# Two of twelve token pairs loaded with four tokens to a partition, and a new order of all steps, in a fused gated-attention and feed-forward kernel

## The chip, the core and the metric

The kernel runs on one core of a Trainium2 chip. The metric is device microseconds (us) from the first to the last instruction of one execution, with what lies around it. Five engines work beside each other, each through its own queue in order: TensorE (PE in the profile; its weight loads are PEld), VectorE (DVE), ScalarE (ACT), GpSimd (POOL) and SyncE (SP), which issues nearly all DMAs. A step that waits holds up everything behind it on its engine.

## What is computed

```
f = 1 / (1 + exp(-f_logit))                          # 4 batches, 8 heads, 768 tokens, 48 channels
for t in range(768):
    state = f[t][:, None] * state + outer(k[t], v[t])  # 48 x 48 for each batch and head
    y[t]  = q[t] @ state
x = y with the heads side by side                    # 3072 tokens x 384
h = x @ w_in                                         # 384 -> 2048
out = (h * cos(h)) @ w_out                           # 2048 -> 384
```

## The kernel before

**Attention.** The recurrence is worked in chunks of 128 tokens, two chunks (256 tokens of one batch) at a time; such a pair is the unit of the loop, and there are twelve, three to a batch. A pair lies on 128 partitions with two consecutive tokens on each, so a chunk takes 64 partitions, and all eight heads lie along each row. `fetch` and `load` (L296) bring f, k, q and v; a run of bytes in DRAM is 2 tokens x 48 channels x 4 bytes = 384 bytes. For pair n the steps are: `ex`, `ln` (L329, L333, ACT) give log(1+exp(-f_logit)), the negative log of the gate; `cum` (L374, L380, PE) sums it along a chunk with a triangular matrix and, with the matrix `half`, over whole chunks; `eb` and `ei` (L391, L395, ACT) take the exponentials of the sums with both signs; `fx`, `fy`, `qa`, `ka` (L347, L344, L341 or L338, L351) correct q and k for the two tokens that share a partition; `qm`, `km` (L404, POOL or DVE) multiply q and k by the decays and write bf16; `vb` and four copies `vt` (L197, a helper that records every copy) bring v to bf16 and into the layout in which the two tokens of a partition are apart. `tq`, `tk` (L435) turn q and k on PE, `qkt` copies them out of PSUM; for pairs 5 to 11 a DMA turns them instead. `sc` (L456) makes the scores, `am` (L461, DVE) masks them, `ps` (L479) makes the outer products of a chunk, `st` (L497) adds the state before and `sz` (L503) scales the sum with the decay of the whole chunk; `y` and `yi` (L531) make the output from the masked scores and from the state, `xe` copies it to the x of the second half.

**Pairs 0 and 1** are cut into two halves of the heads (`HALVES`), so that the first heads can start while the others are still on their way: loads, `ex`, `ln`, `fx`, `cum`, `eb`, `ei`, `qa`, `ka` come in two pieces of 4 heads, named .0 and .1.

**Feed-forward.** Units 0 and 1 take 128 tokens each (both of pair 0), unit 2 the 256 of pair 1, and so on. `h` (L579) multiplies x by w_in into two-bank PSUM tiles of 1024 columns (a unit of 128 tokens has two such tiles, one of 256 has four; a step such as h0.01 is half a tile), `co` (L584, ACT) takes the cosine, `g` (L561, DVE) the product, `o` (L595) multiplies by w_out in four steps for each 128 tokens, `ot` copies the result out and `out` (L606) stores it. The weights are fetched in eight pieces of 768 KB (`w0.*` of w_in, `w1.*` of w_out, L282) and cast by `wc` on POOL or ACT. h0.01 needs `wc0.1`, h0.00 `wc0.0`, h0.11 `wc0.3`, h0.10 `wc0.2`.

**The order.** ORDER is a list of all 953 steps with the engine and the buffers of each, written out; every engine runs its steps in that order. The letter after the colon names the engine (T is PE, S ACT, V DVE, G POOL, Y SP), the digits the slots or the PSUM banks. `zf` steps (L264, 54 of them, ZEROS) are matmuls of zeros that fill TensorE's idle time before the feed-forward part runs dense. PSUM has eight banks, and a step that writes a bank waits until its last reader is through.

Of the kernel before, what the change touches and what calls it, by code (L numbers as in the profile page):

```python
# [16 lines left out]
C = 128  # L17
# [8 lines left out]
HALVES = (0, 1)  # L26
VHALVES = ()
# [12 lines left out]
zf12:T2 zf13:T2 zf14:T2 zf15:T2 zf16:T2 zf17:T2 tk0.0:T2 eb0.1:S0 ex1.0:S ln1.1:S1 ln1.0:S fx1.0:S  # L40
q0.1:Y0 q0.0:Y v0:Y0 fx1.1:S eb0.0:S qa0.1:V zqk.1:V qm0.1:V vb0:S0 f3:Y2 k1.1:Y1 km0.1:V qa0.0:V
zf18:T3 cum1.1:T3 zf19:T4 zf20:T4 zf21:T4 tq0.1:T0 cum1.0:T1 qm0.0:G zsz.2:G eb1.0:S1 vt0.3:S2
k1.0:Y ei1.0:S0 ex3:S zf22:T4 zf23:T4 zf24:T4 zf25:T4 zf26:T4 ps0.1:T4,5 ps0.0:T tk0.1:T v1:Y1 f2:Y0
qkt0.1:V0 eb1.1:S ln3:S0 ei1.1:S ka1.0:G q1.0:Y0 tq0.0:T ka1.1:G km1.1:G0 zvt.1:G vt0.0:S ad3:G1
vt0.1:G q1.1:Y vb1:S1 qkt0.0:V1 vt0.2:G zsz.1:G ex2:S w0.1:Y0 w0.0:Y1 k3:Y0 q3:Y1 w0.3:Y2 ln2:S1
vt1.2:S1 fy3:S zf27:T6 zf28:T6 zf29:T6 zf30:T6 zf31:T6 zf32:T6 sc0.0:T0 sz0.01:V2 sz0.00:V w0.2:Y3
ad2:G0 vt1.0:G km1.0:V vt1.3:G wc0.1:G am0.0:V0 zf33:T6 zf34:T6 yi0:T4 sc0.1:T2 am0.1:V1 st0.11:V
sz0.11:V3 wc0.0:G k2:Y1 zf35:T6 zf36:T6 zf37:T6 zf38:T6 ps1.1:T6,7 tk1.0:T0 ps1.0:T zf39:T1 zf40:T1
zf41:T1 cum3:T1 fy2:S ei3:S0 fx3:S ka3:G eb3:S2 vt1.1:S fx2:S km3.0:G1 qa3:G qm3.0:G km3.1:G qm3.1:G
w1.0:Y0 qa1.0:V st0.10:V qa1.1:V qm1.0:V wc0.2:G ka2:G q2:Y2 tk1.1:T2 zf42:T3 zf43:T3 y0:T3 tq1.0:T  # L50
xe0.1:S0 sz0.10:V st1.00:V st1.01:V qm1.1:V v2:Y1 zf44:T5 zf45:T5 zf46:T5 zf47:T5 zf48:T5 tq1.1:T
cum2:T1 sz1.00:V1 qkt1.0:V0 eb2:S0 xe0.0:S ei2:S1 qkt1.1:V1 km2.0:G0 km2.1:G zf49:T5 sc1.0:T4
sz1.01:V zf50:T0 zf51:T0 sc1.1:T2 h0.01:T0 st1.11:V sz1.11:V2 am1.1:V0 wc1.0:G qa2:G zf52:T6 zf53:T6
h0.00:T co0.0:S0 qm2.1:G am1.0:V1 h1.01:T2 h1.00:T co1.0:S1 y1:T6,4 yi1:T g0.0:V1 xe1.1:V1 st1.10:V
qm2.0:G vb2:G1 sz1.10:V g1.0:V4 w1.2:Y3 xe1.0:S tk3.0:T5 h2.01:T0 tq3.0:T w1.3:Y0 qkt3.0:V0 v3:Y0
f4:Y0 h2.10:T6 h2.00:T sc3.0:T4 tq3.1:T2 tk3.1:T h2.11:T wc1.2:G wc1.3:G vt2.1:G1 wc0.3:S vb3:G0
# [48 lines left out]
o16.3:T sc10.0:T2 co10.2:S1 out13:Y ot16:S3 g10.2:V sc10.1:T4 ps11.1:T1 vt11.0:G vt10.3:G2 ps11.0:T
qa11:G vt11.1:S qm11.1:G st11.01:V tq11.1:Y2 sz11.01:V2 am10.0:V0 am10.1:V1 h10.31:T6 o17.3:T0
# [82 lines left out]
def describe(nc, cpool, ppool, q, k, v, f_logit, moe_w_in, moe_w_out, out):  # L189
# [19 lines left out]
    if nc is not None:  # L209
# [3 lines left out]
        for t in (incl, strict, half):  # L213
            nc.vector.memset(t, 0.0)
# [503 lines left out]
```

## Time and profile before

| what | value |
|---|---|
| median of 3 runs | 183.65 us (183.43 to 183.81) |
| the profiled execution | 183.05 us |
| its span, first to last instruction | 181.3 us |
| mean granted TensorE clock | 0.998 |
| PE busy | 174.0 us, 96% of the span |
| DVE, ACT, POOL busy | 138.2, 130.7, 109.2 us |

Matmuls are pipelined and their ends are modelled, so the busy time of a few short matmuls counts some latency twice; the distance between the starts of two groups is the surer measure. A row of the timeline is: start, duration, engine, line, operation, tiles, count, and in brackets the idle time before it and what ended that.

### The profile page before, as it was taken

The numbers are of one execution on the slowest core, as the hardware profiler recorded it, in microseconds if no ns is written. First come the engines' busy times: TensorE is split into PE (matmuls) and PEld (weight loads), VectorE is DVE, ScalarE is ACT, GpSimd is POOL, SyncE is SP. The second block draws the span as 40 slices with busy tenths as digits, with TensorE's granted clock in tenths as the row PEclk, the third lists the DMA queues.
The fourth block names the chain that finished last, engine by engine and source line by source line (L and its number), as shares of the span: only waits on it lengthen the run. The fifth ranks groups of instructions, "written<-read, shape, count | busy, mean of one in ns | idle before, by whom it ended". The sixth has DMA issues, their size and how long they took to land.

```text
span 181.3 us, 5818 instructions
## 1 busy us (share of the span) xinstructions
PE 174.0 (96%) x2464; PEld 124.2 (69%) x2464; DVE 138.2 (76%) x206; ACT 130.7 (72%) x187; POOL 109.2 (60%) x139
## 2 busy tenths in 40 slices
PE   7999788999999999999999999999999999999992
PEld 2555357785677876778657886658788767786661
DVE  5359988898685989897999698689888994466260
ACT  3985988778877999989997899769768452473221
POOL 4229889999969996989755968790799000000000
PEclk9999999999999999999999999999999999999999
DMA  6999999999999945996889999749929400110313
GB/s 141 261 261 263 346 304 318 293 283 281 317 264 241 270 77 128 253 230 133 125 162 317 189 242 253 175 125 244 216 85 197 90 4 0 38 52 4 130 43 130
DMA packets 72282, 33.93 MB, mean 187 GB/s; under 512 B 65344, under 2 KB 70720, under 8 KB 72256
## 3 DMA queue, kind: packets, MB, share of 16 engines
q1 hardware_dynamic: 71584, 33.27, 76.6%
q8 instruction: 19, 0.31, 0.7%
q10 hardware_dynamic: 672, 0.30, 0.6%
q14 instruction: 7, 0.06, 0.1%
HBM read 25.17 MB, written 4.72 MB: 165 GB/s over the span
## 4 chain that ended last, share of the span: by engine, by line
PE 80%; DMA 8%; SPq 5%; DVE 3%; POOL 1%; issue 1%; ACT 1%; POOLq 0%
PE ps L595 35%; PE ps L579 32%; DMA k<-in_k_dram 5%; PE ps L531 5%; SPq L296 3%; PE ps L456 3%; DMA v<-in_v_dram 3%; PE ps L479 2%; DVE g L561 1%; SPq L282 1%; PE ps L435 1%; PE ps L374 1%; DVE am L461 1%; POOL qk L404 1%; POOL k L351 1%
## 5 line engine op out<-in xcount | busy, mean ns | idle before, releaser
L561 DVE TENSOR_TENSOR g<-ps,co 128x1024 bf16<-128x1024 f32 x48 | 61.3, 1311 | 15.8 <-ACT co L584 14.8
L595 PE MATMUL ps<-w_out_bf,g 128*128 128x384 bf16 x384 | 68.9, 326 | 0.0
L579 PE MATMUL ps<-x,w_in_bf 128*128 128x256 bf16 (+1 forms) x624 | 68.2, 264 | 0.6 <-DVE x L197 0.5
L584 ACT ACTIVATE co<-ps,halfpi 128x1024 bf16<-128x1024 f32 x48 | 52.7, 1113 | 20.0 <-PE ps L579 19.8
L579 PEld LDWEIGHTS <-w_in_bf 128*128 128x128 bf16 x624 | 56.3, 98 | 9.3 <-DVE x L197 0.7
L595 PEld LDWEIGHTS <-g 128*128 128x128 bf16 x384 | 36.0, 98 | 21.5 <-issue 0.3
L461 DVE TENSOR_TENSOR am<-ps,pmask 128x1024 bf16<-128x1024 f32 x24 | 28.7, 1218 | 5.0 <-PE ps L456 4.8
L404 POOL TENSOR_TENSOR qk<-k,bi 128x384 bf16<-128x384 f32 x22 | 22.0, 1010 | 5.4 <-ACT bi L391 4.7
L404 POOL TENSOR_TENSOR qk<-q,b 128x384 bf16<-128x384 f32 x21 | 20.9, 1004 | 2.7 <-DVE q L338 2.1
L197 POOL COPY vt<-vb 64x384 bf16<-64x384 bf16 x33 | 16.7, 507 | 1.6
L264 PE MATMUL ps<-zero 128*128 128x512 bf16 x54 | 16.1, 426 | 1.2 <-DVE zero L203 1.2
L503 DVE TENSOR_TENSOR sz<-ps,b 64x192 bf16<-64x192 f32 x40 | 14.1, 353 | 2.5 <-PE ps L479 1.6
L341 POOL TENSOR_TENSOR q<-f,q 128x384 f32<-128x384 f32 x10 | 10.0, 1000 | 8.3 <-DMA q<-in_q_dram 6.1
L363 POOL TENSOR_TENSOR sp<-ls 128x384 bf16<-128x384 f32 x10 | 10.2, 1015 | 7.7 <-ACT ls L333 5.9
L329 ACT ACTIVATE f<-f 128x768 f32<-128x768 f32 (+1 forms) x14 | 10.4, 746 | 4.5 <-DMA f<-in_f_logit_dram 4.4
L351 POOL TENSOR_TENSOR k<-k,f 128x384 f32<-128x384 f32 (+1 forms) x12 | 11.1, 930 | 4.2 <-DMA k<-in_k_dram 4.2
L497 DVE TENSOR_TENSOR ps<-ps,sz 64x192 f32<-64x192 f32 x32 | 11.7, 366 | 1.9 <-PE ps L479 0.8
L197 ACT COPY ot<-ps 128x384 f32<-128x384 f32 (+1 forms) x14 | 6.1, 453 | 8.7 <-PE ps L595 8.7
L197 ACT CAST x<-ps 128x384 bf16<-128x384 f32 x12 | 5.5, 479 | 5.9 <-PE ps L531 5.9
L456 PE MATMUL ps<-qkt 48*64 48x128 bf16 (+1 forms) x304 | 8.7, 219 | 1.0 <-DVE sz L503 0.8
L197 DVE CAST x<-ps 128x384 bf16<-128x384 f32 x12 | 6.4, 552 | 4.0 <-PE ps L531 3.8
L264 PEld LDWEIGHTS <-zero 128*128 128x128 bf16 x54 | 4.9, 105 | 6.1 <-issue 2.2
(64 smaller groups left out, 167.5 us busy)
## 6 DMA issues: line engine op xcount, KB each, us to landing
v<-in_v_dram SPq DMA_DIRECT2D x12, 384.0 KB, 6.0
out_dram<-ot SPq DMA_DIRECT2D x22, 192.0 KB, 2.1
f<-in_f_logit_dram SPq DMA_DIRECT2D x10, 384.0 KB, 6.0
k<-in_k_dram SPq DMA_DIRECT2D x10, 384.0 KB, 6.7
q<-in_q_dram SPq DMA_DIRECT2D x10, 384.0 KB, 6.7
g<-in_moe_w_in_dram SPq DMA_DIRECT2D x4, 768.0 KB, 7.6
g<-in_moe_w_out_dram SPq DMA_DIRECT2D x4, 768.0 KB, 5.8
k<-in_k_dram SPq DMA_DIRECT2D x4, 192.0 KB, 4.5
```

What stands on the lines that cost most here:

```text
L197: (nc.scalar.copy if e == "ACT" else eng(e).tensor_copy)(out=o, in_=i)
L264: G.step(f"zf{i}", ("PE",), lambda e, dump=dump: nc.tensor.matmul(dump.ap, lhsT=zero[:, 0:128], rhs=zero, start=True, stop=True), writes=[ ...
L351: eng(e).tensor_mul(out=w.ap[:, :, 0, :], in0=w.ap[:, :, 0, :], in1=t.ap[:, :, 0, :])
L404: G.step(f"{nm}{n}.{u}", ("POOL", "DVE") if cut else ("POOL",), lambda e, u=u, j=j, src=src, dec=dec: eng(e).tensor_mul(out=qkp[u][j].ap[: ...
L456: nc.tensor.matmul(o[t0:t1, r, 2 * a + g, :].rearrange("p (e n) -> p e n", e=2), lhsT=wide[s, t0 // 64, :] if turned else wide[s].rearrang ...
L461: G.step(f"am{n}.{u}", ("DVE",), lambda e, u=u, sc=sc: nc.vector.tensor_mul(out=am[u].ap.rearrange("p r b n -> p (r b) n"), in0=sc.ap.rear ...
L497: nc.vector.tensor_add(out=view()[s], in0=view()[s], in1=S0.ap[s, :, r, :])
L503: eng(e).tensor_mul(out=new.ap[s, :, r, :].rearrange("p (u a) n -> p u a n", u=2), in0=view()[s].rearrange("p (u a) n -> p u a n", u=2), i ...
L561: nc.vector.tensor_mul(out=o.rearrange("p b (n e) -> p b e n", e=2), in0=ph.ap.rearrange("p (b e n) -> p b e n", e=2, n=64), in1=co.ap.rea ...
L579: nc.tensor.matmul(ph.ap[:, i * T:(i + 1) * T].rearrange("p (g t) -> p g t", t=C), lhsT=w_in_bf[:, kk, f0:f0 + 128], rhs=xa[:, :, kk, :], ...
L584: G.step(f"co{m}.{j}", ("ACT",), lambda e, ph=ph, co=co: nc.scalar.activation(out=co.ap, in_=ph.ap, func=AF.Sin, bias=halfpi), reads=[ph], ...
L595: nc.tensor.matmul(po.ap[:, 0:DM], lhsT=gT.ap[:, j, i * C:(i + 1) * C], rhs=w_out_bf[:, j, :], start=(po.first and j == 4 * s), stop=(po.f ...
```

## The change

It has four parts.

1. **Layout of pairs 0 and 1** (`QUADS`, new function `lead4`). Four consecutive tokens lie on a partition, so a run in DRAM is 768 bytes and a chunk of 128 tokens takes 32 partitions. Heads 0 to 3 of both chunks lie on partitions 0 to 63, heads 4 to 7 on 64 to 127. f, k, q and v of these pairs come as two loads of 192 KB each, one for each half of the partitions (16 loads; before, f, k and q came in two loads each and v in one, 14 in all).
2. **Sums on TensorE.** `cum` sums for each of the four tokens of a partition with its own triangle (`incl4` where the other token counts in, else `strict4`), 8 matmuls of 192 columns for two tokens, and 8 small ones for the totals. So `fx`, `qa`, `ka` are gone for these pairs, `ex` and `ln` are one step each for a pair, and `eb`, `ei` write 384 columns each (two tokens, a half pair), into the slot of f and into two slots of `ot`. `et` is the small exponential of the totals. `tm` spreads the totals with a mask.
3. **v and the state on TensorE.** `vq` spreads v with 16 matmuls against columns of the identity into one two-bank PSUM tile, and one copy `vt` (on DVE in the order) takes it out; before, four copies on ACT and POOL did that. `st` becomes `si`: 8 matmuls that add the state before into the PSUM of the outer products, with `sz` after it on all 128 partitions.
4. **A new order** of all steps, 914 of them, with 32 `zf` instead of 54. The pair-2-to-11 code is the same, the `cut` branches are gone, `gate` takes the number of tokens to a partition.

The new functions, cut:

```
load(...): out=val.ap.rearrange("p h e d -> p (h e d)").rearrange("p (h x) -> p h x", x=e*D),
           in_=tok.rearrange("h (p e) d -> p h (e d)", e=e)
fetch(..., quad): for u in range(2): load(f"{kind}{n}.{u}", whole.part(lambda a: a[64*u:64*u+64]), ..., 4*u, 4*u+4, 4)

def cum(x):                                     # lead4: x = 0, 1: tokens 2x and 2x+1
    for y in range(2):
        for e in range(4):
            matmul(pc[x].ap[:, HB*y:HB*y+HB], lhsT=incl4 if e <= 2*x+y else strict4, rhs=sp4()[:, e, :, 0:D], ...)
    if x == 0:
        for a in range(2):
            for e in range(4):
                matmul(<totals, 4 columns>, lhsT=sp4()[:, e, 2*a:2*a+2, :], rhs=quarter, ...)

def spread(e):                                  # vq
    for g in range(2):
        for u in range(2):
            for x in range(4):
                matmul(pv.ap[32*x:32*x+32, 512*g+HB*u:512*g+HB*u+HB], lhsT=ident[:, t], rhs=vb4()[:, x], ...)

def carry(e):                                   # si
    for u in us:
        for i in range(4):
            matmul(ps[g].ap[t, at(u):at(u)+HB//2], lhsT=ident[:, t], rhs=S0.ap[:, 2*u:2*u+2, i//2, :], ...)
```

The start of each queue in the new order (only the steps that the prediction speaks of):

```
SP   f0.1 f1.1 v0.1 v0.0 k0.1 k0.0 f1.0 q0.0 q0.1 k1.0 q1.0 v1.0 k1.1 q1.1 f3 v1.1 f2 w0.1 w0.0 w0.3 w0.2 q3 w1.2 k3 w1.3 k2 q2 f4 w1.0 w1.1
ACT  f0.0 ex0 ln0 ei0.0 ei0.1 eb0.0 ex1 eb0.1 et0 ln1 et1 eb1.0 ei1.1 ei1.0 eb1.1 ex3 vb1 ex2 ln2 ln3 fy3 qkt1.1 eb2 ei2 fx3 ei3 eb3 wc0.0 fx2 co0.0 co1.0 xe1.0
DVE  km0.0 zsp.1 vt0 qm0.0 zsz.0 tm0 qm0.1 sz0.01 qkt0.0 qkt0.1 sz0.00 qm1.0 am0.0 sz0.10 sz0.11 am0.1 qm1.1 xe0.0 qkt1.0 xe0.1 sz1.00 sz1.01 am1.1 sz1.10 sz1.11 am1.0 vt1 xe1.1 g0.0 g1.0 zsp.2 g0.1 g2.0 g2.2 g2.3 g1.1 qkt3.0 qkt3.1 g2.1
POOL zqk.2 vb0 km0.1 km1.1 tm1 zsz.1 km1.0 ad2 ad3 wc0.1 wc0.3 wc0.2 qa3 qm3.0 wc1.2 ka3 km3.1 km3.0 qm3.1
PE   zf0-12 cum0.0 cum0.1 vq0 zf13 tk0.0 zf14-17 ps0.0 tk0.1 ps0.1 tq0.0 zf18 tq0.1 cum1.0 cum1.1 sc0.0 sc0.1 si0.1 zf19-20 tk1.1 zf21 si1.0 yi0 tq1.0 zf22-23 tq1.1 tk1.0 ps1.1 y0 zf24-26 cum2 zf27-29 cum3 ps1.0 zf30 sc1.1 zf31 si1.1 sc1.0 vq1 h0.01 h0.00 h1.00 h1.01 yi1 y1 h0.11 h0.10 h2.01 h2.00 h2.21 h2.20 h2.30 h2.31 h1.11 h1.10 o0.2 tq3.0 h2.10 h2.11 tk3.1 tk3.0 tq3.1 o3.2 sc3.0 o2.3 o2.2 o1.3 sc3.1 o3.3
end  DVE ot20 ot23.0 ot22.1; ACT ot23.1 ot22.0 (before: ACT ot23.0 ot23.1)
```

In the order before, the same places read:

```
SP   f0.1 k0.0 k0.1 f1.1 f1.0 q0.1 q0.0 v0 f3 k1.1 k1.0 v1 f2 q1.0 q1.1 w0.1 w0.0 k3 q3 w0.3 w0.2 k2 w1.0 q2 v2 w1.2
PE   ... zf49 sc1.0 zf50-51 sc1.1 h0.01 zf52-53 h0.00 h1.01 h1.00 y1 yi1 tk3.0 h2.01 tq3.0 h2.10 h2.00 sc3.0 tq3.1 tk3.1 h2.11 h2.20 h2.21 h0.11 sc3.1 h0.10 h1.11 h1.10 h2.30 tk2.1 tk2.0 h2.31 o2.0 tq2.1 tq2.0 o0.0 o3.0 o1.0
```

More of the change, by code (lines that the diff above doesn't have):

```diff
@@ L40 @@
[L40 to L56, printed above, removed]
@@ L116 @@
-out22.1:Y o23.2:T o23.0:T o23.1:T ot23.0:S3 out23.0:Y ot23.1:S out23.1:S
+zvt.2:V zsz.3:V zqk.1:V f0.1:Y0 zsp.0:V f0.0:S ex0:S ln0:S0 f1.1:Y1 v0.1:Y0 v0.0:Y k0.1:Y0 k0.0:Y
+f1.0:Y q0.0:Y0 q0.1:Y zf0:T0 zf1:T0 zf2:T0 zf3:T0 zf4:T0 zf5:T0 zf6:T0 zf7:T0 zf8:T0 zf9:T0 zf10:T0
+zf11:T0 zf12:T0 cum0.0:T0 ei0.0:S0 cum0.1:T1 ei0.1:S1 k1.0:Y1 q1.0:Y1 eb0.0:S v1.0:Y1 k1.1:Y q1.1:Y
+ex1:S eb0.1:S et0:S0 zqk.2:G vb0:G0 zvt.0:V km0.0:V1 zsp.1:V vq0:T2 km0.1:G vt0:V0 qm0.0:V ln1:S1
+zf13:T4 tk0.0:T4,5 zsz.0:V tm0:V0 qm0.1:V zf14:T6 zf15:T6 zf16:T6 zf17:T6 ps0.0:T2,6 tk0.1:T ps0.1:T
@@ new lines @@
+f3:Y2 v1.1:Y tq0.0:T zf18:T1 tq0.1:T cum1.0:T0 et1:S0 eb1.0:S cum1.1:T1 f2:Y0 sz0.01:V0 qkt0.0:V0
+qkt0.1:V1 sz0.00:V sc0.0:T4 w0.1:Y0 w0.0:Y1 ei1.1:S1 ei1.0:S0 eb1.1:S ex3:S vb1:S0 w0.3:Y2 qm1.0:V1
+km1.1:G tm1:G1 zsz.1:G sc0.1:T2 si0.1:T am0.0:V0 sz0.10:V3 sz0.11:V km1.0:G ex2:S ln2:S0 ad2:G1
+zf19:T0 zf20:T0 tk1.1:T1,0 ln3:S1 zf21:T4 si1.0:T6 w0.2:Y3 yi0:T4 ad3:G0 am0.1:V1 qm1.1:V wc0.1:G
+wc0.3:G tq1.0:T wc0.2:G zf22:T5 zf23:T5 tq1.1:T tk1.0:T ps1.1:T2 y0:T5 fy3:S xe0.0:V0 qkt1.1:S0
+qkt1.0:V1 xe0.1:V q3:Y0 zf24:T5 zf25:T5 zf26:T5 cum2:T1 zf27:T5 zf28:T5 zf29:T5 cum3:T4 ps1.0:T
@@ L506, in pair @@
             for r in range(2):
[L507 to L508 removed]
+                G.step(f"sz{n}.{g}{r}", ("DVE",), lambda e, r=r: decay(e, r), reads=[half_of[r], bt], writes=[new.part(None)])
+        for g in gs:
+            new = Val(szS)
+            (state4 if quad else state2)(g, new, before[g])
             state[b] = new
```

416 lines of the change are left out of this document (252 added, 164 removed).

## The prediction

> **What bounds the kernel now.** First the stages: busy time of each engine by windows (columns: window, length, PE busy with its count, PEld, DVE, ACT, POOL, clock, DMA share, GB/s).
>
> ```profile
> 5.00:16.00 11.00, 10.85 (x131) 5.88 (x129) 6.10 (x13) 9.82 (x25) 4.56 (x6) 1.00 1.28 263
> 18.00:20.00 2.00, 1.31 (x43) 0.71 (x38) 1.76 (x6) 1.94 (x3) 1.26 (x4) 1.00 1.01 353
> ...
> 44.00:60.00 16.00, 16.00 (x262) 11.25 (x257) 11.19 (x21) 12.44 (x18) 13.65 (x20) 1.00 1.14 268
> ```
>
> ```profile
> 80.00:100.00 20.00, 20.00 (x378) 14.65 (x377) 18.39 (x26) 18.50 (x29) 14.72 (x18) 1.00 0.88 190
> ```
>
> From 44 us on TensorE has no idle time, and neither layout nor step count changes there. So the end moves by what is gained or lost before 44, plus the tail. Before that PE looks as busy, but with what?
>
> ```profile
> L264 PE MATMUL ps<-zero 128*128 128x512 bf16 x52 | 15.5, 428 | 1.2 <-DVE zero L203 1.2
> ```
>
> 52 of the 54 zero matmuls lie before 24.9 us: the lead-in is a chain through DMA, ACT, DVE and POOL, and PE waits in it. The timeline shows where the lead-in ends and where it is caught up:
>
> ```profile
> 24.91 0.84 PE L579 MATMUL ps<-x,w_in_bf 128*128 128x128 bf16 x12
> ...
> 26.03 2.17 PE L579 MATMUL ps<-x,w_in_bf 128*128 128x128 bf16 x36
> 26.90 1.11 ACT L584 ACTIVATE co<-ps,halfpi 128x1024 bf16<-128x1024 f32 x1 [0.77 <-PE ps L579]
> ...
> 28.10 1.33 DVE L561 TENSOR_TENSOR g<-ps,co 128x1024 bf16<-128x1024 f32 x1 [0.65 <-POOL qk L404]
> ```
>
> ```profile
> 41.69 2.11 PE L595 MATMUL ps<-w_out_bf,g 128*128 128x384 bf16 x12
> 43.74 0.40 PE L456 MATMUL ps<-qkt 48*128 48x128 bf16 x8
> ```
>
> h0.01 starts at 24.91, the first g at 28.10, and at 43.8 PE has done all of h0 to h2, y1, the turns of pairs 3 and 2, sc3 and sixteen second-half matmuls (o2.0, o0.0, o3.0, o1.0). That point is my yardstick: when does the new order have as much done?
>
> **The durations that I use** (line, engine, what, count, busy, mean ns; groups before 44 us).
>
> ```profile
> L329 ACT ACTIVATE f<-f 128x768 f32<-128x768 f32 x2 | 1.7, 838 | 1.9 <-DMA f<-in_f_logit_dram 1.9
> L333 ACT ACTIVATE ls<-f 128x768 f32<-128x768 f32 x2 | 1.7, 842 | 0.0
> L197 ACT CAST vb<-v 128x768 bf16<-128x768 f32 x2 | 1.7, 832 | 1.0 <-DMA v<-in_v_dram 1.0
> L395 ACT ACTIVATE bi<-ps 128x384 f32<-128x384 f32 x2 | 1.0, 493 | 0.0
> L197 ACT COPY qkt<-ps 128x1024 bf16<-128x1024 bf16 x2 | 2.0, 1007 | 0.2 <-PE ps L435 0.2
> L197 ACT CAST w_in_bf<-g 128x1536 bf16<-128x1536 f32 x1 | 1.5, 1484 | 0.0
> L584 ACT ACT_TABLE_LOAD x1 | 1.3, 1283 | 0.0
> ```
>
> ```profile
> L404 POOL TENSOR_TENSOR qk<-k,bi 128x384 bf16<-128x384 f32 x6 | 6.2, 1033 | 4.9 <-ACT bi L391 4.7
> L363 POOL TENSOR_TENSOR sp<-ls 128x384 bf16<-128x384 f32 x2 | 2.2, 1080 | 0.7 <-ACT ls L333 0.7
> L197 POOL CAST w_in_bf<-g 128x1536 bf16<-128x1536 f32 x3 | 4.3, 1464 | 0.1
> ```
>
> ```profile
> L561 DVE TENSOR_TENSOR g<-ps,co 128x1024 bf16<-128x1024 f32 x8 | 10.2, 1314 | 0.7 <-POOL qk L404 0.6
> L461 DVE TENSOR_TENSOR am<-ps,pmask 128x1024 bf16<-128x1024 f32 x6 | 7.1, 1218 | 1.3 <-PE ps L456 1.3
> L197 DVE COPY qkt<-ps 128x1024 bf16<-128x1024 bf16 x6 | 3.9, 678 | 2.2 <-PE ps L435 2.2
> L503 DVE TENSOR_TENSOR sz<-ps,b 64x192 bf16<-64x192 f32 x8 | 2.8, 354 | 0.2
> L497 DVE TENSOR_TENSOR ps<-ps,sz 64x192 f32<-64x192 f32 x6 | 2.2, 366 | 0.3
> L404 DVE TENSOR_TENSOR qk<-q,b 128x384 bf16<-128x384 f32 x3 | 1.6, 532 | 0.0
> L197 DVE CAST x<-ps 128x384 bf16<-128x384 f32 x1 | 0.5, 543 | 0.0
> ```
>
> ```profile
> 4.26 0.94 ACT L329 ACTIVATE f<-f 128x384 f32<-128x384 f32 x2 [1.73 <-DMA f<-in_f_logit_dram]
> ...
> 8.69 0.33 PE L374 MATMUL ps<-sp,incl 128*128 128x192 bf16 x2
> ...
> 8.86 0.24 PE L380 MATMUL ps<-half,sp 128*128 128x2 bf16 x4
> ...
> 8.96 0.81 PE L264 MATMUL ps<-zero 128*128 128x512 bf16 x3
> ...
> 28.13 0.63 PE L531 MATMUL ps<-am,vt 128*32 128x128 bf16 x32
> 28.59 0.51 PE L531 MATMUL ps<-qkt,sz 128*32 128x128 bf16 x24
> ```
>
> **Part by part.** *Loads.* Now the queue of loads is a straight line in time. In the chain of waits v0, eight half loads behind f0, lands at 5.10 + 5.53 = 10.63:
>
> ```profile
> 5.10 5.53 DMA v<-in_v_dram
> ```
>
> 192 KB at 263 GB/s is 0.75 us, and 4.7 for f0 (the second `ex` of the row above starts there) plus 8 x 0.75 is 10.7, so the rule holds: each load costs its bytes, in the order of issue. Of a load into half the partitions the trace has no row. From above: 384-byte runs went at 263 GB/s, the weights' longer ones at 353; the 768-byte runs could reach the latter, 0.56 us for 192 KB. From below: half the partitions, half of 263, 1.5 us. I take the nearest row, the same bytes in 384-byte runs, 0.75 us. From 4.7 on, k0 is complete at 8.5 (5 loads on), q0 at 10.7, f3 at 15.9, v1 at 16.7, f2 at 18.2, and at 353 GB/s w0.1 20.4, w0.0 22.6, w0.3 24.9, w0.2 27.1. f2 goes into f0's slot, which now holds decays until qm0.1 (12.2); SP waits there with the weights queued behind it, hidden as long as the transfers issued ahead (to 16.7) run on.
>
> *Sums.* cum0.0 has 8 matmuls of 192 columns and 8 small ones. Two took 0.17 us from 8.69 to 8.86, four small ones 0.10 to 8.96: 0.9 us, and 0.7 for cum0.1, each with 0.2 to the reader. Before, a pair took 0.54, so PE gets about 1.0 more a pair; the 22 zero matmuls that go, at 0.21 each (three in about 0.6), give 4.7 back. The added vq is 16 matmuls in four column groups: y's 32 took 0.46 from start to start, 14 ns each for 128 columns, so 0.35. An si takes 0.1 by the same pitch, ps twice its matmuls, a turn 8 instead of 4; I take 0.5, 0.25 to 0.4. All of it lies in time that zeros filled; if no gap were left, PE's own work from 6.4 to h0.01 would add up to some 16.5 us with its 19 zeros, to 22.9, so PE is not what sets 24.7. ps of these pairs takes four banks instead of two, which is hidden while the feed-forward part has none yet.
>
> *ACT* drops `fx` (four of 192 columns) and its three vt copies of these pairs, and gets four exponentials of 384 columns a pair for four of 192, qkt1.1 (1.0) and wc0.0 (1.5): it is full from 13.7 on, and what stands late in its queue is late in the kernel. POOL drops three vt, ka1 and pair 3's steps ahead of the casts, so all of w_in is cast by 28.6 instead of 33.1:
>
> ```profile
> 31.64 1.47 POOL L197 CAST w_in_bf<-g 128x1536 bf16<-128x1536 f32 x1
> ```
>
> *DVE* loses ka, qa and 6 `st` (6 x 0.37 = 2.2 us), wins vt0, vt1 (not shown from PSUM at 768 columns; between x at 0.54 and g at 1.31, I take 1.0 each) and two `xe` (0.54 each): no net gain. vt0 stands ahead of qm0.0 in DVE's queue and ends at 10.25 (vq0 at 8.6, zsp.1); q0, at 10.7, hides it; were q there sooner, qm0.0, tq0, cum1 and all of pair 1 would wait for vt0. DVE's set-up gets about 14 short instructions, some 1.5 us, hidden under f0's arrival and `ex`, `ln`; if it isn't, up to 0.5 us is lost. A `gate` that writes every fourth element: from nothing to 0.1 us each, I take nothing, as the elements are as many.
>
> **The walk**, by the queues in their order (us):
>
> | step | waits for | ends |
> |---|---|---|
> | ex0, ln0 (ACT) | f0 4.7 | 6.4 |
> | cum0.0, cum0.1 | ln0 | 7.5, 8.2 |
> | ei0.1, eb0.0, ex1, eb0.1, ln1 | cum0.1 | 11.7 |
> | km0.1 (POOL), ps0.0 (PE) | ei0.1 8.8 | 9.8, 10.4 |
> | qm0.0, qm0.1 (DVE) | q0 10.7 | 11.3, 12.2 |
> | tq0.1, cum1.0, cum1.1 | qm0.1 | 14.4 |
> | et1, eb1.0, ei1.1, ei1.0, eb1.1 | cum1 | 15.95 |
> | ex3, vb1 | f3, v1 | 17.7 |
> | ex2, ln2, ln3 | **f2 18.2** | 20.8 |
> | fy3, qkt1.1, four eb/ei, fx3 | | 24.8 |
> | wc0.0, fx2, table load | w0.0 22.6 | 26.3, 28.1 |
> | ad2, ad3, wc0.1 (POOL) | ln2 19.95 | 23.6 |
> | am0.0 to xe0.1 (DVE) | sc0.0 14.8 | 22.6 |
> | cum3, ps1.0, sc1.1, si1.1, sc1.0, vq1 | ad3 22.1 | 24.7 |
> | h0.01, h0.00, h1.0 | wc0.1; wc0.0 | 28.5 |
> | am1.1, sz, am1.0, vt1 (DVE) | sc1.1 | 27.8 |
> | y1, xe1.1, g0.0 | vt1 | 29.4, 30.0, 31.4 |
>
> Each row adds the durations above to the later of its queue and its wait. So h0.01 starts at 24.7, 0.2 before 24.91, but g0.0 at 30.0, 1.9 after 28.10: y1 and xe1.1 stand ahead of it. What follows is denser, since no h waits for a cast any more. Tiles come free every 1.31 us with DVE: g1.0 32.7, g0.1 34.2, g2.0 35.5, g2.2 36.8, g2.3 38.1, g1.1 39.4, the two qkt3 40.8, g2.1 42.1. PE follows: h0.1 30.8, h2.0 32.2, h2.2 33.5, h2.3 34.8, h1.1 36.2, o0.2 36.9, h2.1 38.4, turns 39.1, o3.2 39.8, sc3.0 40.5, o2.3, o2.2, o1.3 42.5, sc3.1 42.8, o3.3 43.45.
>
> ```profile
> 46.34 3.36 PE ps L595 x20
> ```
>
> By 43.45 six o steps are done where before had four at 43.80: two at 4 x 0.168 make 1.34; the turns of pair 2 (0.9, the two groups of 0.45 before 41.85) are still owed. That is 0.44 us of work and 0.35 of time: **0.8 us gained**. Tail:
>
> ```profile
> 178.04 0.54 ACT L197 COPY ot<-ps 128x192 f32<-128x192 f32 x2 [4.74 <-PE ps L595]
> 178.62 0.36 ACTq L606 DMA_DIRECT2D out_dram<-ot  x1
> ```
>
> Two copies in a row on ACT become one each on ACT and DVE: 0.2 gained. Sum -1.0 on the profiled execution's 183.05, so 182.05; it lies 0.6 below the median of the runs, so I forecast **182.65** for the median.
>
> **Rivals.** *Half-partition loads are slow.* [...] Place: ex2 on ACT, which stands at f2 already at 0.75 us a load; 14 of them lie ahead of f2 after f0, so every 0.1 us above that costs 1.4 us at ln2, ad3 and all below. At half of the best rate of the rows, 353/2, a load takes 1.11 and the price is 5.0; half way there, at 0.93, 2.5: **185.2**, slower. It decides from 0.82 a load on, where the 1.0 is gone. For it: DMA is never idle from 5 to 20 us. Against: w0.3 and w0.2 stand earlier in the queue. [...] Chance 0.33.
>
> *Loads near 353 GB/s.* Then f2 is there at 15.5, ex2 starts behind vb1 at 17.7 and gains 0.5, and the weights come 2.7 earlier; with turns and cum at the short end another 0.6: **181.6**. Chance 0.17.
>
> *DVE hides it.* g0.0 starts 1.9 late, and am, g and qkt keep DVE full to 42; if PE gets no o steps into those gaps, because o0.2 or sc3 wait for banks a tile longer (1.31), 0.8 - 1.31 leaves it **0.3 slower to even, 183.7**. Chance 0.14.
>
> *The clock drops.* With 22 zeros fewer PE has more gaps; the first ten zero matmuls took 0.43 each, twice the 0.21 of later ones, and a spell of 4.5 us at that speed costs about 2: 184.7. In before gaps up to 0.8 us did no harm. Chance 0.04.
>
> ```profile
> 1.19 4.45 PE L264 MATMUL ps<-zero 128*128 128x512 bf16 x10 [1.19 <-DVE zero L203]
> ```
>
> **Numbers.** The forecast has 0.32, from 182.0 to 183.5. A run tells 0.2% (0.37 us) from no change. Faster: the forecast but 0.03, and the quick loads, 0.46 (0.29 + 0.17); within 0.2%: 0.03 and 0.07 of the DVE case, 0.10; slower: slow loads 0.33, 0.07, 0.04, 0.44. The range 181.3 to 185.6 reaches into both load cases and leaves out the slow end beyond 0.96 us a load.
>
> **What would show it.** DMA at 5 to 14 us: 263 GB/s or more is right, under 240 the first rival. ex2 starting by 18.3 with DMA f as releaser; cum0.0 by 6.5; h0.01 by 24.9 and g0.0 at 30; PE without idle from 31. Wrong would be a wait on q0 beyond 10.7, ACT idle ahead of ex3, vb1 or ex2 by over 1 us, or PE idle after 44, where I allow the new order none.

## The result and the profile after

| | before | after |
|---|---|---|
| median | 183.60 us (5 runs, 183.43 to 183.81) | 195.22 us (5 runs, 194.29 to 195.38) |
| ratio | | 1.0622, 95% interval 1.0596 to 1.0648 |
| profiled execution, span | 183.05, 181.3 us | 195.02, 193.0 us |
| mean granted clock | 0.998 | 0.979 |

The kernel became 11.6 us slower; 182.65 was forecast, with 185.6 as the upper end. One later run (experiment 8, 185.47 us, 2.4% above its fastest) counts as slow and is left out of its ratio. First the stages of after, by the same windows view as in the prediction (window, length, busy time and count of PE, PEld, DVE, ACT, POOL, then clock, DMA share, GB/s).

```profile
5.00:10.00 5.00, 3.13 (x44) 2.12 (x42) 1.25 (x6) 3.05 (x5) 0.96 (x2) 1.00 1.13 221
10.00:15.00 5.00, 4.06 (x119) 2.77 (x120) 3.76 (x10) 2.02 (x4) 1.24 (x1) 1.00 1.13 218
...
20.00:25.00 5.00, 3.81 (x102) 2.40 (x102) 2.08 (x4) 3.45 (x5) 0.89 (x1) 0.61 1.06 375
...
36.00:44.00 8.00, 5.55 (x59) 4.50 (x56) 8.00 (x5) 4.29 (x4) 7.77 (x9) 1.00 0.91 236
44.00:60.00 16.00, 11.60 (x115) 7.49 (x116) 15.93 (x13) 12.73 (x15) 7.49 (x12) 1.00 0.88 198
60.00:180.00 120.00, 120.00 (x1844) 90.22 (x1843) 99.08 (x136) 86.66 (x118) 70.24 (x85) 1.00 0.72 154
```

Three places differ from what was expected. The loads run at 218 to 221 GB/s where before had 263. The clock falls to 0.61 between 20 and 25 us. And from 36 to 60 us, where PE was to be dense from 31 on, PE is busy for 17.15 of 24 us while DVE is full (23.93). In the kernel before, PE had no gap to speak of there; its row for 36 to 44 us:

```profile
36.00:44.00 8.00, 7.97 (x103) 6.12 (x100) 7.36 (x7) 6.60 (x8) 7.92 (x8) 1.00 1.04 290
```

From 60 us PE has no idle time in after, so what was lost lies ahead of that. What fills DVE is seen in the groups of its instructions: all of `g`, and those from 62 us on (count, busy us, mean ns).

```profile
L670 DVE TENSOR_TENSOR g<-ps,co 128x1024 bf16<-128x1024 f32 x48 | 69.3, 1502 | 9.7 <-ACT co L693 9.6
```

```profile
L670 DVE TENSOR_TENSOR g<-ps,co 128x1024 bf16<-128x1024 f32 x40 | 50.5, 1308 | 9.7 <-ACT co L693 9.6
```

and the same line in the window up to 62 us:

```profile
L670 DVE TENSOR_TENSOR g<-ps,co 128x1024 bf16<-128x1024 f32 x8 | 18.8, 2472 | 0.0
```

The shape is the same in both, 128x1024 from PSUM to bf16; the eight gates of units 0 to 2, which write every fourth element, take 2.47 us instead of 1.31. That is 8 x 1.16 = 9.3 us on the engine that is full. PE's waits between 24 and 180 us say who stood behind it (us in total, times, longest):

```profile
PE ps L688 <- DVE g L670: 3.3, 4, 1.2
PE ps L515 <- DVE qkt L193: 1.3, 1, 1.3
PE ps L704 <- DVE g L670: 0.9, 1, 0.9
PE ps L486 <- DVE g L670: 0.8, 1, 0.8
...
PE ps L515 <- DVE g L670: 0.5, 1, 0.5
```

These five make 6.8 us, as much as PE idles between 36 and 60 (24 - 17.15), and all of them end with a `g` or with a copy that stood behind `g` in DVE's queue.

The timeline dates the steps of the walk (start, length, engine, line; in brackets the wait before):

```profile
5.36 0.84 ACT L325 ACTIVATE f<-f 128x768 f32<-128x768 f32 x1 [2.53 <-DMA f<-in_f_logit_dram]
...
22.32 0.84 ACT L405 ACTIVATE f<-f 128x768 f32<-128x768 f32 x1 [0.43 <-DMA f<-in_f_logit_dram]
```

```profile
30.62 2.84 PE L688 MATMUL ps<-x,w_in_bf 128*128 128x128 bf16 x48
```

```profile
34.88 4.77 DVE L670 TENSOR_TENSOR g<-ps,co 128x1024 bf16<-128x1024 f32 x2
39.70 11.57 DVE L670 TENSOR_TENSOR g<-ps,co 128x1024 bf16<-128x1024 f32 x5
52.30 2.46 DVE L670 TENSOR_TENSOR g<-ps,co 128x1024 bf16<-128x1024 f32 x1
```

`ex0` starts at 5.36 (forecast 4.7), `ex2` at 22.32 (18.2), h0.01 at 30.62 (24.7), g0.0 at 34.88 (30.0), and g2.1 ends at 54.8 (42.1). So 4.9 us of the delay are there when the gates begin and 7.8 come while they run.

### The profile page after: what moved, and what is told of

It is laid out like the page before. It is cut to its first block, busy times and chain, and to the rows that moved or that the text cites. A ratio compares the mean times of both kernels' runs of the same rounds, so it can differ in the third digit from the quotient of the medians.

```text
span 193.0 us, 6129 instructions
## 1 busy us (share of the span) xinstructions
PE 175.5 (91%) x2618; PEld 126.3 (65%) x2618; DVE 147.2 (76%) x220; ACT 128.9 (67%) x176; POOL 103.3 (54%) x132
## 4 chain that ended last, share of the span: by engine, by line
PE 73%; DVE 10%; DMA 10%; issue 2%; SPq 2%; ACT 1%; DVEq 0%
PE ps L704 31%; PE ps L688 27%; DVE g L670 8%; DMA k<-in_k_dram 6%; PE ps L640 5%; DMA q<-in_q_dram 4%; PE ps L515 3%; PE ps L554 2%; PE ps L271 2%; SPq L303 2%; PE ps L438 1%; PE ps L486 1%; ACT w_in_bf L193 1%; DVE qkt L193 1%; DVE am L520 1%
## 5 line engine op out<-in xcount | busy, mean ns | idle before, releaser
L670 DVE TENSOR_TENSOR g<-ps,co 128x1024 bf16<-128x1024 f32 x48 | 69.3, 1502 | 9.7 <-ACT co L693 9.6
L693 ACT ACTIVATE co<-ps,halfpi 128x1024 bf16<-128x1024 f32 x48 | 52.9, 1113 | 27.3 <-PE ps L688 18.2
L456 POOL TENSOR_TENSOR qk<-k,bi 128x384 bf16<-128x384 f32 x20 | 19.7, 1002 | 1.1 <-ACT bi L447 0.6
L193 POOL COPY vt<-vb 64x384 bf16<-64x384 bf16 x28 | 13.9, 501 | 6.0 <-PE ps L640 3.0
L271 PE MATMUL ps<-zero 128*128 128x512 bf16 x32 | 11.8, 490 | 3.6 <-DVE am L520 1.4
L422 POOL TENSOR_TENSOR k<-k,f 128x384 f32<-128x384 f32 x10 | 10.0, 1002 | 5.7 <-DMA k<-in_k_dram 5.6
L193 DVE COPY ot<-ps 128x384 f32<-128x384 f32 (+1 forms) x12 | 6.2, 522 | 8.3 <-PE ps L704 7.4
L604 DVE TENSOR_TENSOR ps<-ps,sz 64x192 f32<-64x192 f32 x26 | 9.5, 367 | 3.3 <-PE ps L554 2.5
L610 DVE TENSOR_TENSOR sz<-ps,b 64x192 bf16<-64x192 f32 x32 | 11.1, 353 | 0.7
L405 ACT ACTIVATE f<-f 128x768 f32<-128x768 f32 x10 | 8.4, 839 | 2.3 <-DMA f<-in_f_logit_dram 2.3
L447 ACT ACTIVATE bi<-ps 128x384 f32<-128x384 f32 x10 | 4.9, 492 | 6.4 <-PE ps L442 6.3
```

The source lines that it names most:

```text
L193: (nc.scalar.copy if e == "ACT" else eng(e).tensor_copy)(out=o, in_=i)
L271: G.step(f"zf{i}", ("PE",), lambda e, dump=dump: nc.tensor.matmul(dump.ap, lhsT=zero[:, 0:128], rhs=zero, start=True, stop=True), writes=[ ...
L422: eng(e).tensor_mul(out=w.ap[:, :, 0, :], in0=w.ap[:, :, 0, :], in1=t.ap[:, :, 0, :])
L456: G.step(f"{nm}{n}.{u}", ("POOL",), lambda e, u=u, j=j, src=src, dec=dec: eng(e).tensor_mul(out=qkp[u][j].ap[:, :, :, 0:D], in0=swap(src.a ...
L610: eng(e).tensor_mul(out=new.ap[s, :, r, :].rearrange("p (u a) n -> p u a n", u=2), in0=view()[s].rearrange("p (u a) n -> p u a n", u=2), i ...
L670: nc.vector.tensor_mul(out=o.rearrange("p b (n e) -> p b e n", e=E), in0=ph.ap.rearrange("p (b e n) -> p b e n", e=E, n=C // E), in1=co.ap ...
```

## Experiments

Theory: two causes, the gate's write at a step of four elements and the slow loads of half the partitions. Rivals: the fallen clock; something in the new sums or the order. A ratio compares with runs of the kernel before on the same chip, with its 95% interval in brackets; a difference in us to after is one of medians that may come from two chips.

**1. The gate alone, out of the kernel after.** Units 0 to 2 keep PSUM's order in g, and the store puts the rows in order:

```
+ if E == 4:
+     tensor_mul(out=o, in0=<ph, in order>, in1=<co, in order>); return
- dma_start(out=out[r0:r0 + C, c0:c1], in_=oc.ap)
+ rows = out[r0:r0 + C, c0:c1].rearrange("(n e) c -> e n c", e=4)      # units 0 to 2
+ for x in range(4): dma_start(out=rows[x], in_=oc.ap[32 * x:32 * x + 32])
```

> The changed kernel, but the gate product g of units 0 to 2 is written in the order in which it lies in PSUM (unit steps), and the store puts the rows in order, in four pieces of 32 rows. Theory GATE (the product written in steps of four elements, 2.48 instead of 1.31 us, eight times on a full VectorE, makes the larger part of the 11.6 us): g back to about 1.3 us and 186 to 188.5 us. Rival LEAD-IN (the loads into half the partitions and the clock drop make nearly all, and PE could have used the waits on g for other work): 193 us or more. Neither: if g stays above 2 us, it is not the write step.

Measured: 188.39 us, ratio to before 1.0293 (1.0229 to 1.0356): 6.8 us less than after, 6.0 by the two ratios. The eight gates in the window up to 62 us, and the stage in which PE had been idle:

```profile
L671 DVE TENSOR_TENSOR g<-ps,co 128x1024 bf16<-128x1024 f32 x8 | 9.5, 1211 | 0.2
```

```profile
36.00:44.00 8.00, 8.00 (x144) 7.28 (x137) 6.99 (x8) 6.75 (x8) 7.77 (x9) 1.00 0.98 254
44.00:60.00 16.00, 16.00 (x211) 10.37 (x212) 13.74 (x20) 13.85 (x19) 9.74 (x14) 1.00 0.95 218
```

PE's idle time from 36 to 60 us is gone with it.

**2. The gate alone, put into the kernel before**, units 0 to 2 in steps of four (their tokens come out in another order; the work is the same):

```
- def gate(gv, ph, co, T):      ... e=2, n=64
+ def gate(gv, ph, co, T, E):   ... e=E, n=C // E       # E = 4 if m < 3 else 2
```

> The kernel before, with one edit: g of units 0 to 2 is written in steps of four elements instead of two (which leaves the tokens of these units in another order; the work is the same). GATE: g 2.4 to 2.5 us there, VectorE was full from 28 to 43 us, so most of 8 x 1.17 us shows: 190 to 193 us. LEAD-IN: TensorE finds other work, under 186 us.

Measured: 190.85 us, ratio 1.041 (1.0388 to 1.0433), 7.5 us more than before on the same chip. Its gates up to 62 us:

```profile
L561 DVE TENSOR_TENSOR g<-ps,co 128x1024 bf16<-128x1024 f32 x8 | 19.0, 2475 | 0.6 <-POOL qk L404 0.6
```

No load, no sum and no place in the order was touched, so the price belongs to the write alone.

**3. The loads alone**: the sixteen early loads bring the same number of bytes in the same 768-byte runs, but two heads of 512 tokens to all 128 partitions instead of four heads of 256 to 64. They are other tokens than the reference's, the same ones for both pairs, so only the time counts.

```
- load(name, whole.part(lambda a: a[64*u:64*u + 64]), src, b, c, 4*u, 4*u + 4, 4)
+ dma_start(out=<a[:, 4*u:4*u + 4], 128 partitions>, in_=src[b, 4*u:4*u + 2, 0:4*C, :] as "h (p e) d -> p h (e d)")
```

> The changed kernel, but each of the 16 loads of pairs 0 and 1 brings its 192 KB in runs of 768 bytes to all 128 partitions (two of the four slots a row) instead of 64; it reads other tokens, so only the time counts. GATE: 300 GB/s or more from 5 to 12 us, f2 lands at 16 to 17 instead of 22.2, h0.01 starts at 25 to 26 instead of 30.6, and the end moves by about as much: 189.5 to 191.5 us, with g still at 2.48. LEAD-IN: 186 us or less. If the rate stays near 220 GB/s, it is not the number of partitions.

Measured: 190.14 us, ratio 1.0373 (1.0347 to 1.0398), 5.1 us less than after, 4.6 by the two ratios. The windows row of after and then two of this run, `ex2`, and h0.01:

```profile
5.00:20.00 15.00, 10.19 (x213) 6.62 (x212) 8.36 (x21) 7.72 (x15) 4.68 (x6) 1.00 1.16 222
```

```profile
5.00:20.00 15.00, 13.05 (x316) 8.60 (x317) 10.83 (x25) 10.49 (x20) 5.71 (x8) 1.00 1.10 330
...
5.00:10.00 5.00, 4.75 (x57) 2.92 (x56) 2.87 (x9) 2.97 (x6) 1.82 (x2) 1.00 1.06 324
```

```profile
16.81 0.84 ACT L411 ACTIVATE f<-f 128x768 f32<-128x768 f32 x1 [0.38 <-DMA f<-in_f_logit_dram]
```

```profile
24.24 2.84 PE L694 MATMUL ps<-x,w_in_bf 128*128 128x128 bf16 x48
```

Up to 20 us this run moves part of the weights too, so the loads' own rate is better read from 5 to 10 us: 324 GB/s, where after had 221. 192 KB (196,608 bytes) take 0.89 us at 221 to 222 GB/s and 0.61 at 324. SP's issues don't set that rate: in after the loads of k and v landed 5.7 us (median) after they were issued, so several were under way at any time. Whether it helped the rate that both pairs read the same tokens was not tried apart. h0.01 starts 6.4 us earlier.

**4. The clock**: nine zero matmuls more (ZEROS 41), six of them ahead of `tk1.1` and three behind `zf21`.

> The changed kernel with nine zero matmuls more between 16.7 and 20 us, where TensorE waits and after which its clock falls to half from 21.1 to 28.0 us. If the clock drop costs time of its own: the clock stays at 1.0 and the end comes 1.5 to 3 us earlier, 192 to 193.7 us. If it lies beside the waits for the late loads: within 0.5 us of 195.2, whatever the clock does.

Measured: 194.95 us, ratio 1.0636 (1.0606 to 1.0667). The windows of after, then of this run (the clock is the third number from the end):

```profile
22.00:28.00 6.00, 5.34 (x93) 3.04 (x94) 1.62 (x3) 5.13 (x8) 3.35 (x3) 0.50 1.05 385
```

```profile
22.00:28.00 6.00, 4.26 (x130) 2.71 (x129) 1.83 (x5) 5.48 (x9) 2.95 (x3) 1.00 1.05 381
```

```profile
29.85 2.87 PE L688 MATMUL ps<-x,w_in_bf 128*128 128x128 bf16 x48
...
34.54 4.77 DVE L670 TENSOR_TENSOR g<-ps,co 128x1024 bf16<-128x1024 f32 x2
```

The clock held, and h0.01 came 0.8 us earlier (29.85 for 30.62) although f2 was later in this run (`ex2` at 23.25 for 22.32): from `ex2` to h0.01 it took 6.60 us instead of 8.30. Little of it reached the end: g0.0 began 0.3 us earlier, and the time is the same within the noise (0.3 us less by the medians, none by the ratios). What the fallen clock costs when f2 comes at the same time, these runs don't tell.

**5. Both causes undone** (the edits of 1 and 3 together).

> The kernel after with both edits of before this: the gate of units 0 to 2 writes at unit step (the rows put in order by the store, in four pieces of 32 rows) and the sixteen early loads bring the same bytes to all 128 partitions (other tokens than the reference's, so the output is not the reference's). If gate and loads are the two causes and add up, 188.4 less some 5 is left: 182 to 184 us, the forecast's 182.65 among them, the eight gates at 1.21 us, h0.01 near 24.3 and PE without idle after 31. If something else of the change costs as well (the sums on TensorE, the spreading of v, the order), it stays at 185.5 or more with PE idle between 36 and 60.

Measured: 183.95 us (182.51 to 184.94 in 10 runs), ratio 1.0001 (0.9968 to 1.0034). That is the upper end of what was expected. PE's one wait after 44 us was this (units 0 to 2 at unit step, tokens as in 3):

```profile
PE ps L521 <- DMA qkt<-qk: 0.9, 1, 0.9
```

The transfers of qkt stand in SP's queue with the stores, of which units 0 to 2 now have four for one (experiment 8 tries this).

**6. What the step of the write costs.** In the kernel before, six units of 256 tokens each get another form of `g`, of one shape and so each with a line of its own:

```
+ m == 4: out=o                                  (write at unit step)
+ m == 5: e=4   m == 6: e=8   m == 9: e=16       (write every 4th, 8th, 16th element)
+ m == 7: e=4   m == 8: e=2, all three operands as "p b n e"   (write in order, read at a step)
```

> The kernel before, with another form of gate in each of six units of 256 tokens, all 128x1024 from PSUM to bf16: unit step in unit 4, elements 8 bytes apart in unit 5 (every fourth), 16 bytes in unit 6, the standard one's result written in order with reads 128 bytes apart in unit 7 (fours) and 256 bytes apart in unit 8 (twos), 32 bytes in unit 9; the tokens of units 4, 5, 6 and 9 come out in another order. If the step of the write decides: 1.2 us at unit step, 1.31 at 4 bytes, 2.47 at 8, at least 2.47 at 16 and 32, and 1.2 to 1.4 for the two that write in order. If any step on either side costs the same, these two take 1.3 (twos) and 2.47 (fours). If the cost grows with the step, 16 and 32 bytes take 4 us and more.

Units 4, 5, 6 and 9 come out with their tokens in another order. The groups of `g` in one run (L574 the standard form, L562 unit step, L564 8 bytes, L566 16, L572 32, L568 and L570 in order with fours and twos):

```profile
L574 DVE TENSOR_TENSOR g<-ps,co 128x1024 bf16<-128x1024 f32 x24 | 30.9, 1318 | 12.4 <-ACT co L595 11.5 <-issue 0.7
L566 DVE TENSOR_TENSOR g<-ps,co 128x1024 bf16<-128x1024 f32 x4 | 18.9, 4825 | 0.7 <-ACT co L595 0.7
L572 DVE TENSOR_TENSOR g<-ps,co 128x1024 bf16<-128x1024 f32 x4 | 17.6, 4585 | 0.0
L564 DVE TENSOR_TENSOR g<-ps,co 128x1024 bf16<-128x1024 f32 x4 | 10.0, 2556 | 0.1
L568 DVE TENSOR_TENSOR g<-ps,co 128x1024 bf16<-128x1024 f32 x4 | 7.5, 1902 | 0.3 <-ACT co L595 0.3
L570 DVE TENSOR_TENSOR g<-ps,co 128x1024 bf16<-128x1024 f32 x4 | 4.9, 1219 | 1.7 <-ACT co L595 1.6
L562 DVE TENSOR_TENSOR g<-ps,co 128x1024 bf16<-128x1024 f32 x4 | 4.7, 1208 | 0.0
```

1.21 us at 2 bytes, 1.32 at 4, 2.56 at 8, 4.83 at 16, 4.59 at 32: up to 4 bytes nearly free, then the time doubles with the step until it is 16 bytes. The length of the innermost loop is not what counts: it is 32 at 8 bytes (2.56 us) and 2 in L570 (1.22). With the loops exchanged, so that the write is in order, twos cost 1.22 and fours 1.90; the strided read of fours costs too, which "1.2 to 1.4" had missed; why it does and that of twos does not, was not tried.

**7. Two queues for the loads.** Gate as in 1; the loads of heads 0 to 3 are issued by ACT, so that both halves of the partitions are under way together.

```
- SP  ... v0.1 v0.0 k0.1 k0.0 f1.0 q0.0 q0.1 k1.0 q1.0 v1.0 k1.1 ...
+ SP  ... v0.1 k0.1 q0.1 k1.1 q1.1 ...      ACT f0.0 v0.0 k0.0 f1.0 q0.0 ex0 ln0 ei0.0 ei0.1 eb0.0 k1.0 q1.0 v1.0 ...
```

> The kernel after with the gate at unit step, and the early loads of the heads 0 to 3 (the lower 64 partitions) issued by ACT, those of the heads 4 to 7 by SP, so that loads of both halves are under way together; the output is the reference's. If a load of 64 partitions is slow because it has half of the partitions to write to, two at a time come to 270 GB/s or more between 5 and 12 us, h0.01 starts by 27.5 and the time is 183 to 186 us. If the rate belongs to the packets or to HBM, it stays at 205 to 225 GB/s and the time at 187.5 to 190. ACT pays about 0.5 us for each of its seven issues; if these come late on its path the time gains less than 2 us although the rate is up.

Measured: 189.72 us, ratio 1.0333 (1.0294 to 1.0372), no faster than with one queue (1.0293 in experiment 1). The windows of this run, then of after:

```profile
6.25:9.40 3.15, 2.06 (x24) 1.48 (x23) 0.00 (x0) 2.02 (x4) 0.66 (x1) 1.00 1.13 272
12.00:20.00 8.00, 4.83 (x127) 3.44 (x116) 4.28 (x10) 4.34 (x10) 2.26 (x4) 1.00 1.20 208
```

```profile
6.25:9.40 3.15, 2.22 (x41) 1.92 (x40) 0.00 (x0) 1.87 (x4) 0.82 (x1) 1.00 1.13 233
```

While both queues had loads, 272 GB/s against 233; later 208. From 5 to 12 us, the stretch that was named ahead of the run, it is 239 against 225, short of the 270. ACT paid for it: its five issues of 0.6 to 0.7 us (one in after) lasted until 4.98, and the load of its function table came only behind them, so `ex0` moved from 5.36 to 6.30.

```profile
5.01 1.28 ACT L756 ACT_TABLE_LOAD   x1 [5.01 <-DMA f<-in_f_logit_dram]
```

`ex2` began at 22.42, in experiment 1 at 22.44, so nothing was gained where it counts; the mean clocks of the four runs, 0.962 to 0.982, may have cost time too. From 5 to 12 us the second queue gained 6% (239 for 225), in the two rows of the shorter stretch 17%, still far from the 324 into 128 partitions (experiment 3). 239 lies between the two cases expected, 270 or more and 225 at most, so the run doesn't settle what limits a load into 64 partitions.

**8. Both causes undone, stores in one piece** (as 5, rows of units 0 to 2 left in another order).

> The run with both edits, with the rows of units 0 to 2 stored in one piece for each 128 (so they stand in another order, and the loads bring other tokens). PE's one wait after 44 us in that run was 0.9 us for a transfer of qkt on SP's queue; if the four-piece stores held it up there, that wait goes and the time is 182.4 to 183.3 us, with the forecast's 182.65 inside. If the rest belongs to the change, it stays at 183.6 to 184.3.

Measured: 182.24 us, ratio 0.9907 (0.9873 to 0.9941), a little below the 182.4 to 183.3 expected. PE's wait for qkt is not in the trace any more, so the stores in four pieces cost 1.7 us in experiment 5. Whether experiment 1 paid for them too is not shown: its trace has no such wait.

**9. The gate in order, in the kernel before**: the loops exchanged, all else and the result as they were.

```
- tensor_mul(out=o.rearrange("p b (n e) -> p b e n", e=2), in0=ph.ap.rearrange("p (b e n) -> p b e n", e=2, n=64), in1=...)
+ tensor_mul(out=o.rearrange("p b (n e) -> p b n e", e=2), in0=ph.ap.rearrange("p (b e n) -> p b n e", e=2, n=64), in1=...)
```

> The kernel before, its gate alone changed: the loops over the tokens of an output block exchanged, so that it writes in order and reads 256 bytes apart; same result. 48 gates at 1.22 instead of 1.31 us, 4.5 us of DVE in all. PE is the bound from 44 us on and idles some 2 us before it for DVE; if only the eleven gates before 44 us count, 0 to 0.6 us are gained: 182.8 to 183.6 us. If the whole sum counted, 179. If the reads disturb the others on PSUM, 184 or more.

Measured: 183.22 us in 12 runs, ratio 0.9974 (0.9958 to 0.9989). It computes the same and is 0.3% faster than before: the 48 gates fall from 61.3 to 57.4 us of DVE, but PE is the bound.

**10. The same edit in the kernel after** (fours and twos in order).

> The kernel after, the gate alone changed in the same manner, with fours in units 0 to 2 and twos from there on; same result. The eight gates at 1.90 instead of 2.47 us: 4.6 us of DVE; unit step saved 10.1 us of DVE and 6.8 of the time, so by the same share 3.1 us: 191.3 to 192.7 us. If the forty gates of twos counted too (0.1 us each), 188 to 190.

Measured: 191.45 us, ratio 1.041 (1.0375 to 1.0445): 3.8 us for one exchanged loop. The eight gates:

```profile
L670 DVE TENSOR_TENSOR g<-ps,co 128x1024 bf16<-128x1024 f32 x8 | 14.6, 1879 | 0.0
```

**11. The clock once more, with the gate out of the way** (1 and 4 together).

> The kernel after with the gate at unit step, and nine zero matmuls more between 16 and 20 us. Without them the granted clock was 0.5 to 0.67 from 20 to 36 us and h0.01 began at 32.3. If the clock stays at 1.0: were it hidden by the loads, as it was beside the slow gate, the time changes by 0.5 us at most (187.9 to 188.4); if it is on the path now that DVE isn't, h0.01 begins near 29.9 and the time is 186 to 187 us.

Measured: 188.49 us, ratio 1.0263 (1.0232 to 1.0295), where experiment 1 had 188.39 and 1.0293. h0.01 began at 29.45 as the second theory wanted, and the median did not change, as the first said; by the ratios 0.6 us were gained, within the intervals. But the runs without the added zeros spread more (187.72 to 190.39), and the profile of experiment 1 is of the slowest of them. There the clock was still down up to 36 us; its row, then that of this run, and its g0.0:

```profile
30.00:36.00 6.00, 5.53 (x95) 4.63 (x93) 3.75 (x5) 3.72 (x5) 5.12 (x6) 0.67 1.12 333
```

```profile
30.00:36.00 6.00, 4.78 (x123) 4.43 (x121) 3.28 (x4) 4.63 (x6) 5.12 (x5) 1.00 1.12 330
```

```profile
37.37 2.35 DVE L671 TENSOR_TENSOR g<-ps,co 128x1024 bf16<-128x1024 f32 x2
```

`ex2` began at 22.44 and 22.68, but g0.0 at 37.37 and, with the zeros, at 35.11; the spans are 188.5 and 186.1 us. So a clock that stays down until 36 us cost some 2.3 us in these two profiles. The other three runs of experiment 1, at mean clocks of 0.98 to 1.00 (the slowest had 0.961), took 187.72 to 188.78, so the median shows nothing of it.

**12. The tail.** On top of 9, the last two copies on DVE and ACT as in after (`ot23.0:V3` for `ot23.0:S3`).

> The kernel before with its gate writing in order, and of the last two copies (two halves of one result) the first on DVE and the second on ACT, as in the kernel after. In the forecast the two ran beside each other and gained 0.2 us. In the profile of after the last copies on the two engines each waited 0.5 us for the one before on the other engine, and from the end of the last matmul to the end of the span it took 3.3 us there and before alike. If they wait for each other here too, the copies start 0.4 to 0.5 us apart, and the time is that of the run without this edit, 183.2 us, within 0.2. If they run beside each other, they start within 0.1 us of each other and the time is 183.0.

Measured: 183.40 us, ratio 0.9987 (0.9976 to 0.9998); no gain. The DVE copy, then the ACT copy:

```profile
178.37 0.36 DVE L197 COPY ot<-ps 128x192 f32<-128x192 f32 x1 [1.33 <-PE ps L595]
```

```profile
178.76 0.32 ACT L197 COPY ot<-ps 128x192 f32<-128x192 f32 x1 [5.13 <-DVE ot L197]
```

ACT waits for DVE: both read one result in one bank, and the second starts when the first is done. The kernel lifts the order between steps on two engines only where they use different banks (`apart`, L754 of after), so the wait may be the program's own; whether the chip would ask for it was not tried.

## Why the prediction was wrong

- **The step that failed**: "A `gate` that writes every fourth element: from nothing to 0.1 us each, I take nothing, as the elements are as many." It was 1.16 us each, 9.3 us on DVE, and the walk gave each `g` 1.31 us where 2.47 were needed. It was worth 6.8 us in the kernel after (experiment 1, 6.0 by the ratios, with a gate that is 0.1 us shorter still than the old one) and 7.5 in the kernel before (2). The element count was the wrong measure, and the rows had a sign of it: `am`, of the same shape and written in order, took 1.218 us, the old `gate`, writing every second, 1.311 (mean of all 48). A price of 0.09 at a step of two was no reason to put the upper bound at 0.1 for a step of four; the trace had no row of such a write, so the bound had to lie far away.
- **Loads**, the second term that was mis-sized: 0.75 us for a load of 192 KB was taken; 0.89 was measured. The first rival named the half partitions, the place (`ex2` on ACT) and the direction; in experiment 3, with the same bytes and runs in twice the partitions, the rate rose from 221 to 324 GB/s. No run shows the half rate on which that rival's prices stand (353/2 GB/s, 1.11 us a load; 0.93 half way there): the 221 of after are 0.68 of the 324 into 128 partitions. Of the 4.1 us by which `ex2` was late (22.32 for 18.2), 14 x 0.14 = 2.0 follow from that price and 0.7 from f0 (`ex0` at 5.36 for 4.7); the other 1.4 were not traced. The prediction's own signs of slow loads came true (under 240 GB/s, a wait for q0 until 12.45, ACT idle by 1.86 us ahead of `ex3`); the gate shows only in its last sign, PE idle after 44 us, which the prediction took for a fault of the order.
- **The walk** from `ex2` to h0.01, 6.5 us in the table, was nearly right where the clock held and f2 was late: 6.60 (4) and 6.77 (11). In after it took 8.30, so some 1.7 are the clock's, by one profile each. So h0.01 was 5.9 late: 4.1 by the loads, nearly all the rest by the clock. With the fast loads it took 7.43 at full clock (3): PE reached `cum2` only at 20.12, behind zeros that had waited for `xe0.0`.
- **DVE hides it** was the right place (DVE full from 36 on, PE waiting for tiles) for the wrong reason: a tile did not come free 1.31 us late, but every tile took 2.47.
- **The clock drops**: it did, at 0.50 from 22 to 28 us, for the reason given (fewer zeros while the loads are awaited; nine more held it at 1.00). At the end of after nothing of it is clear of the noise (195.22, with the zeros 194.95; ratios 1.0622 and 1.0636). In the slowest run of experiment 1, where the gate was out of the way and the clock down until 36 us, some 2.3 us were lost, near the 2 of this rival.
- **Confirmed**: the sums (cum0.0 and its totals, 0.87 us from 7.12 to 7.99, 0.9 forecast), `vt0` (0.90; 1.0), no idle time of PE after 60. With both causes undone the kernel came to 0.9907 of before, 1.7 us (8), where 1.0 had been forecast; its loads were faster than the forecast's and its gates 0.1 us shorter than 1.31, so the nearer measure is the second rival's 181.6, 2.0 below before. That the new layout would gain with loads at 263 GB/s has not been shown.
- **Tail**: 0.2 was forecast, nothing came (12); in after, too, each of the last copies waited for the one on the other engine.

```profile
189.76 0.36 DVE L193 COPY ot<-ps 128x192 f32<-128x192 f32 x1 [0.53 <-ACT ot L193]
190.16 0.32 ACT L193 COPY ot<-ps 128x192 f32<-128x192 f32 x1 [0.53 <-DVE ot L193]
```

The sum: after stands 12.6 us above the forecast. Undoing gate and loads one at a time gave 6.8 and 5.1 back, 11.9 together; undoing both with the same stores gave 11.3 (5), and 13.0 with plain stores (8). By the ratios it is 6.0 and 4.6, 10.6 together, against 11.4 and 13.1. Within that spread the two add up, and with both undone nothing of the slowing is left.

## What to carry to other kernels

Ahead of any change of layout, look at the innermost step of every write that follows from it, on the engine that will be full: here the bytes between two elements set the time (1.32, 2.56 and 4.83 us at 4, 8 and 16 bytes, experiment 6), not the number of elements alone. If a strided write can't be avoided, exchange the loops so that the write runs in order, and measure the strided read instead (in after 1.88 us a gate for 2.47, experiment 10). Loads that reach only half of the partitions are to be priced by their own rate (221 GB/s here, where 128 partitions had 324), and each one counts that stands ahead of the first late consumer.

## What the runs showed of the hardware

- A VectorE product of 128x1024 from PSUM to bf16 took 1.21, 1.32, 2.56, 4.83 and 4.59 us at write steps of 2, 4, 8, 16 and 32 bytes (experiment 6); at 8 bytes 2.47 in after and in experiment 2.
- Loads of 768-byte runs went at 221 GB/s into 64 partitions (after) and 324 into 128 (experiment 3); 384-byte runs into 128 had 263 (before). The number of partitions counted more than the run.
- Six microseconds at half the granted clock (after) cost nothing that is clear of the noise (experiment 4); a clock of 0.50 to 0.67 from 20 to 36 us, with the gate out of the way, came with a span 2.4 us longer (profiles of experiments 1 and 11).
